# Routing of tokens in two batches instead of three, with other selection steps, and 26 extra transposes behind the attention

## The chip, the cores and the metric

The kernel runs on one core of a Trainium2 chip. TensorE (PE) multiplies and transposes and writes PSUM only; VectorE (DVE), ScalarE (ACT) and GpSimd (POOL) do the elementwise work; SyncE (SP) issues most DMAs. Every engine works through its own list in order and waits on semaphores. [...] The metric is the device time of one execution in microseconds. It was 711.97 us before, the median of 3 runs (711.90 to 711.98).

## The reference, cut to what matters

Three layers follow each other: windowed attention with sinks, a mixture of 8 experts of which each token takes two, and a gated two-layer network.

```
scores = scale * q @ k.T; keep = is_sink | in_window          # 2 x 8 heads, 768 x 64
x = softmax(where(keep, scores, -1e9)) @ v                    # becomes 1536 tokens x 512
logits = x @ w_gate
noisy = logits + log1p(exp(x @ w_noise)) * noise              # 1536 x 8
top2 = the two largest of a row, with weights softmax(top2)
for e in 8 experts: out[mask] += top2_w * (relu(x[mask] @ w1[e]) @ w2[e])
y = (h * sigmoid(h)) @ w_out, h = out @ w_in                  # 512 -> 2048 -> 512
```

## The kernel before, in words

**Attention.** The 1536 tokens are 12 blocks of 128 rows. A software pipeline goes through 48 positions (12 blocks, 4 pairs of heads each) and 12 more to drain it. At position p TensorE does the scores of p, the transposes of the exponentials of p-2 and the product with V of p-4; ScalarE does the exponentials of p-1 and the high half of the transposed part of p-3, VectorE its low half. Work that belongs to a block hangs on positions in a table, `hooks`, filled by `at(position, function, place)`. Behind the last head of a block come `fin` (the block's rows `xs`, scaled and stored to `x_d`), then `gate_block`: transposes of `xs` (`pm`), their copy `xT`, the gate product `pl`, and its copy `lg`.

**Routing.** When enough blocks have their `lg`, `route` puts a list of small VectorE steps on `drip`; one or two are taken off per position, and in the last 12 positions up to four. BATCHES makes three such lists: blocks 0 to 4, 5 to 8 and 9 to 11. A list forms the noisy logits (`noisy_top`: exponential and logarithm on ScalarE, which need two different activation tables), finds the two largest by `max` and `max_index` per block, turns them into one-hot rows `roh` and `M`, has TensorE count places (`posm`, tile `pp`), and builds two one-hot tables, `Boh` (chunk, multiplied by the token's number on GpSimd) and `Aoh` (place in the chunk). Their product `pz` (`z_part`) is the list of tokens by expert, `idx`. By `idx` GpSimd gathers the rows of the experts.

**The first 128 tokens of expert 0** can be known from the first batch alone. `f_list` finds them, a gather fetches them, `f_xt` transposes them, `f_split` makes high and low halves `fp`, and `f_l1`, `f_relu`, `f_ht`, `f_l2`, `f_out` send them through expert 0's two layers. These pieces wait in `fill` and are put by `do_fill` where TensorE would wait for the routing of the last blocks. `f_rows` then turns the other rows of expert 0, and expert 0's remaining 288 columns start (`l1` in `moe`, tile `ph`).

**Experts.** Each of the 8 experts runs 8 slices f, `l1` of one beside `l2` of the slice before (tiles `ph`, `py`). Between them stand the loads and splits of later weights (`weights_step`), the next expert's rows (`x_pair`, then a DMA transpose `x_turn` on SP's queue, tile `xT`), and the conversion of the last layer's weights (`decode_step`): an even step starts one and loads the one after next (512 KB), an odd step does two VectorE passes and stores an earlier one (256 KB, `win_d`). How many steps stand in a slice is a tuple at the end of the loop in `moe`. All these loads, stores and DMA transposes go through SP's queue in the order of the code.

Of the kernel before, what the change touches and what calls it, by code (L numbers as in the profile page):

```python
# [22 lines left out]
BATCHES = ((0, 5), (5, 9), (9, 12))  # L23
# [21 lines left out]
def setup(ctx, tc, g):  # L45
    nc = tc.nc
    g.B, g.H, g.S, g.D = g.q.shape
    g.N = g.B * g.S
    g.DM = g.H * g.D
    g.NB = g.N // 128  # L50
    g.E = g.w_gate.shape[1]
    g.F = g.w1.shape[2]
    g.F2 = g.w_out.shape[0]
    g.C = 416

    g.CT = [min(128, g.C - 128 * c) for c in range(4)]
# [12 lines left out]
    g.noise_sb = consts.tile([128, g.NB, 8], F32, name="noise_sb")  # L69
    g.ones = consts.tile([128, 128], BF16, name="ones")  # L70
    g.iota8 = consts.tile([128, 8], F32, name="iota8")
    g.M = consts.tile([128, g.NB, 8], BF16, name="M")
    g.Msum = consts.tile([128, 8], BF16, name="Msum")
    g.top8 = consts.tile([128, g.NB, 8], F32, name="top8")
    g.ix = consts.tile([128, g.NB, 8], U32, name="ix")
    g.ef = consts.tile([128, g.NB, 2], F32, name="ef")
# [12 lines left out]
    g.tops = consts.tile([128, 64], F32, name="topsl")  # L89
    g.n_sums = g.n_tops = 0  # L90
    nc.gpsimd.memset(g.sums, 0.0)


def setup_ops(tc, g):

    nc = tc.nc
    p = g.consts
    nc.gpsimd.iota(g.iota8, pattern=[[1, 8]], base=0, channel_multiplier=0,
                   allow_small_or_imprecise_dtypes=True)
    nc.gpsimd.iota(g.iotaq, pattern=[[1, 128]], base=0, channel_multiplier=0,  # L100
                   allow_small_or_imprecise_dtypes=True)
# [118 lines left out]
def noisy_top(tc, g, t, j0, j1):  # L220

    nc = tc.nc
    n = j1 - j0
    J = slice(j0, j1)
    V = nc.vector
    e, u, l, z, dd = (t("r" + c, [8]) for c in "eulzd")
    pre, nz = t("rp", [8]), t("rn", [8])
# [12 lines left out]
    add(lambda: V.tensor_scalar(z, u, 1.0, None, op0=OP.is_equal))  # L240
    add(lambda: V.scalar_tensor_tensor(dd, u, 1.0, z, op0=OP.subtract, op1=OP.add))
    add(lambda: V.tensor_mul(e, e, g.noise_sb[:, J, :]))
    add(lambda: V.reciprocal(dd, dd))
    add(lambda: V.tensor_mul(z, z, e))
    add(lambda: V.tensor_mul(dd, dd, e))
    add(lambda: V.tensor_add(pre, z, g.lg[:, J, 0:8]))
    add(lambda: V.tensor_mul(l, l, dd))
    add(lambda: V.tensor_add(nz, l, pre))
    for j in range(n):
        add(lambda j=j: V.max(g.top8[:, j0 + j, :], nz[:, j, :]))  # L250
    for j in range(n):
        add(lambda j=j: V.max_index(g.ix[:, j0 + j, :], g.top8[:, j0 + j, :], nz[:, j, :]))
    return st


def route(tc, g, wk, ps, j0, j1):
# [6 lines left out]
    def t(name, shape, dt=F32):  # L263
# [3 lines left out]
    pos = t("rpos", [2])  # L267
    sl, pm, cl = (t(c, [2], I32) for c in ("rsl", "rpm", "rcl"))
    st = noisy_top(tc, g, t, j0, j1)
    add = st.append  # L270
    add(lambda: V.tensor_tensor(oh, g.iota8[:, None, None, :].to_broadcast([128, n, 2, 8]),
                                g.ix[:, J, 0:2, None].to_broadcast([128, n, 2, 8]), op=OP.is_equal))
    add(lambda: V.tensor_add(g.M[:, J, :], oh[:, :, 0, :], oh[:, :, 1, :]))

    def posm():
        p = ps.tile([128, n, 8], F32, name="pp", tag="M")
        nc.tensor.matmul(p, g.tri, g.M[:, J, :], start=True, stop=n == 1 and j0 == 0)
        if j0:
            nc.tensor.matmul(p, g.ones, g.Msum[:, None, :].to_broadcast([128, n, 8]), start=False, stop=n == 1)
# [12 lines left out]
    add(lambda: V.tensor_reduce(pos, ps2, axis=AX.X, op=OP.add))  # L292

    add(lambda: V.scalar_tensor_tensor(sl, g.ef[:, J, :], 512.0, pos, op0=OP.mult, op1=OP.add))
# [12 lines left out]
    add(lambda: V.scalar_tensor_tensor(g.sl[:, J, :], g.ef[:, J, :], float(g.C), pos, op0=OP.mult, op1=OP.add))  # L307
    if j1 < g.NB:
        tot = wk.tile([128, 8], F32, name="rtot", bufs=1)

        def msum():
            V.tensor_reduce(tot, g.M[:, J, :].rearrange("p j e -> p e j"), axis=AX.X, op=OP.add)
            if j0:
                V.tensor_add(tot, tot, g.Msum)
            V.tensor_copy(g.Msum, tot)

        add(msum)
# [3 lines left out]
def attention(tc, g):  # L321
# [4 lines left out]
    with ExitStack() as st:  # L326
# [241 lines left out]
        keep_warm(nc, g, ps, "O", 10)  # L568
# [43 lines left out]
        for n in range(NQ):  # L612
# [39 lines left out]
        def f_split(k, scale):  # L652
# [3 lines left out]
            nc.scalar.activation(hi, p, AF.Copy, scale=scale)  # L656
# [45 lines left out]
        def f_out():  # L702
# [6 lines left out]
        work = (fl[0] + fl[1][:2] + [lambda: f_relu(0)] + fl[1][2:] + [lambda: f_ht(0), lambda: f_relu(1)] + f2[0][:2]  # L709
                + [lambda: f_ht(1)] + f2[0][2:] + f2[1] + [f_out])  # L710
# [32 lines left out]
        g.do_fill = do_fill  # L743
# [29 lines left out]
        for p in range(NP + 12):  # L773
# [196 lines left out]
def moe(tc, g, W, wk, ps):  # L970
# [98 lines left out]
    def gates():  # L1069
# [8 lines left out]
            lambda: V.tensor_sub(e2, g.top8[:, :, 1], g.top8[:, :, 0]),  # L1078
# [68 lines left out]
    for i, (e, f) in enumerate(seq):  # L1147
# [241 lines left out]
def flag_steps(tc, g, wk, ps):  # L1389
# [3 lines left out]
    t = wk.tile([128, 5], F32, name="flt", bufs=1)  # L1393
# [3 lines left out]
    def count():  # L1397
        p = ps.tile([128, 13], F32, name="pc", tag="PT")
        nc.tensor.matmul(p[:, 0:8], g.ones, g.Msum, start=True, stop=False, skip_group_check=True)
        for j in range(g.batches[-1][0], g.NB):  # L1400
            nc.tensor.matmul(p[:, 0:8], g.ones, g.M[:, j, :], start=False, stop=False, skip_group_check=True)
        nc.tensor.matmul(p[:, 8:13], g.ones, g.over, start=False, stop=True, skip_group_check=True)
        V.tensor_reduce(t[:, 0:1], p[:, 0:8], axis=AX.X, op=OP.max)
# [6 lines left out]
            lambda: V.tensor_scalar(t[:, 0:1], t[:, 0:1], float(g.C), None, op0=OP.is_gt),  # L1410
            lambda: V.tensor_scalar(t[:, 4:5], t[:, 4:5], 0.5, None, op0=OP.is_gt),
# [28 lines left out]
def general(tc, g):  # L1440
# [4 lines left out]
    with ExitStack() as ctx:  # L1445
# [72 lines left out]
        with ExitStack() as st:  # L1518
# [139 lines left out]
```

## Time and profile before

| | |
|---|---|
| median of 3 runs | 711.97 us |
| the profiled execution, whole | 713.08 us |
| its span on the core | 711.4 us |
| TensorE busy in the span | 667.1 us |
| VectorE, ScalarE, GpSimd busy | 429.3, 337.8, 214.2 us |
| mean granted clock of TensorE | 0.982 |

Rows below come from the profiled execution; its own time lies 1.11 us above the median of the runs, and 1.68 us of it lie around the span. Times in rows are microseconds from the span's start. In a row of the timeline the first two numbers are the start and the duration, `x6` says how many instructions were merged, and a bracket at the end says how long the engine was idle before and what released it.

### The profile page before, as it was taken

What the parts mean: (1) busy time and instruction counts of PE and PEld (TensorE: products, weight loads), DVE (VectorE), ACT (ScalarE), POOL (GpSimd) and SP (SyncE); (2) the same over time, 40 slices, a digit from 0 to 9 for tenths busy, and PEclk for the clock granted to TensorE, in tenths of its full rate; (3) what the DMA queues carried; (4) which work ended last, traced back from release to release, by engine and by line L of the source; (5) the groups of instructions that cost most, each with busy time, mean ns of one, the idle gap of its engine ahead of it and who ended that gap; (6) DMA issues with size and microseconds to landing.
All of it is one profiled execution on the core that took longest, in us unless ns stands there. A gap on an engine that the chain in (4) does not pass through costs nothing.

```text
span 711.4 us, 11618 instructions
## 1 busy us (share of the span) xinstructions
PE 667.1 (94%) x4292; PEld 373.1 (52%) x4292; DVE 429.3 (60%) x1091; ACT 337.8 (47%) x693; POOL 214.2 (30%) x229
## 2 busy tenths in 40 slices
PE   7999889889987999999999999899999999999993
PEld 5677667557543656565555553444444444444441
DVE  5878788737695687878797854756423344232222
ACT  4888868437663555556555441443323223222221
POOL 5868950142162162625252325222100000000000
PEclk9999999799998999999999999999999999999998
DMA  7776710539798989998894514742311011000001
GB/s 153 197 168 178 179 46 24 186 97 242 283 253 309 236 293 270 330 276 267 232 297 155 150 45 135 241 149 67 82 30 59 1 30 29 30 30 1 1 0 65
DMA packets 111682, 103.50 MB, mean 145 GB/s; under 512 B 77312, under 2 KB 77568, under 8 KB 111616
## 3 DMA queue, kind: packets, MB, share of 16 engines
q1 hardware_dynamic: 106016, 86.68, 42.4%
q0 software_dynamic: 4096, 13.11, 6.1%
q10 hardware_dynamic: 1504, 2.88, 1.1%
q8 instruction: 35, 0.57, 0.3%
q14 instruction: 31, 0.25, 0.1%
HBM read 77.29 MB, written 17.30 MB: 133 GB/s over the span
## 4 chain that ended last, share of the span: by engine, by line


## 5 line engine op out<-in xcount | busy, mean ns | idle before, releaser
L1009 PE MATMUL ph<-xT,w 128*128 128x416 f16 (+1 forms) x768 | 141.7, 335 | 8.8 <-DMA win_d<-f 6.6
L1274 PE MATMUL p<-xT,w 128*128 128x512 f16 x576 | 132.2, 379 | 2.1 <-DVE xT L1260 1.4
L1291 PE MATMUL po<-w,h 128*128 128x512 f16 x576 | 132.2, 379 | 0.0
L1025 PE MATMUL py<-h,w 128*128 128x416 f16 (+1 forms) x672 | 124.1, 331 | 3.2 <-DVE h L131 2.7
L937 POOL TENSOR_SCALAR f<-f 128x512 f32<-128x512 f32 x32 | 70.6, 2211 | 157.7 <-ACT f L936 155.6
L1009 PEld LDWEIGHTS <-w 128*128 128x128 f16 x768 | 75.4, 98 | 61.3 <-DMA win_d<-f 7.0
L1277 DVE TENSOR_TENSOR f<-p,f 128x512 f32<-128x512 f32 x48 | 33.1, 691 | 110.9 <-ACT f L1276 109.3
L1025 PEld LDWEIGHTS <-w 128*128 128x128 f16 x672 | 65.7, 98 | 52.6 <-issue 6.1
L1274 PEld LDWEIGHTS <-w 128*128 128x128 f16 x576 | 56.4, 98 | 70.1 <-issue 2.4
L1291 PEld LDWEIGHTS <-h 128*128 128x128 f16 x576 | 56.3, 98 | 67.8 <-DVE h L126 0.3
L1276 ACT ACTIVATE f<-p 128x512 f32<-128x512 f32 x48 | 28.6, 596 | 128.8 <-PE p L1274 126.5
L1012 ACT ACTIVATE h<-ph 128x416 f16<-128x416 f32 (+1 forms) x64 | 31.8, 497 | 52.0 <-PE ph L1009 51.0
L126 DVE SCALAR_TENSOR_TENSOR h<-f,h 128x512 f16<-128x512 f32 x48 | 33.2, 692 | 33.4 <-ACT h L1279 33.4
L126 DVE SCALAR_TENSOR_TENSOR w<-wst,w 128x1024 f16<-128x1024 f32 x38 | 47.2, 1245 | 8.4 <-ACT w L882 8.1
L131 DVE SCALAR_TENSOR_TENSOR h<-ph,h 128x416 f16<-128x416 f32 (+1 forms) x64 | 36.2, 566 | 24.3 <-ACT h L1012 24.3
L1279 ACT ACTIVATE h<-f 128x512 f16<-128x512 f32 x48 | 30.2, 629 | 37.8 <-DVE f L1277 37.8
L482 ACT ACTIVATE P<-pS,mx 128x260 f32<-128x260 f32 (+1 forms) x96 | 43.0, 458 | 1.9 <-DVE mx L473 1.6
L882 ACT ACTIVATE w<-wst 128x1024 f16<-128x1024 f32 x38 | 39.6, 1047 | 0.0
L126 DVE SCALAR_TENSOR_TENSOR rows<-xg,rows 128x512 f16<-128x512 f32 (+1 forms) x36 | 24.8, 688 | 24.2 <-ACT rows L988 24.1
L980 POOL DMA_INDIRECT xg<-x_d,idx x28 | 32.6, 1166 | 20.5 <-DVE topsl L121 13.5
L1064 ACT ACTIVATE yo<-tpy 128x512 f32<-128x512 f32 (+1 forms) x27 | 16.1, 595 | 45.4 <-PE tpy L1054 29.6
L126 DVE SCALAR_TENSOR_TENSOR w<-rows,w 128x1024 f16<-128x1024 f32 x26 | 31.9, 1231 | 4.4 <-ACT w L882 4.1
(254 smaller groups left out, 956.1 us busy)
## 6 DMA issues: line engine op xcount, KB each, us to landing
wst<-in_moe_w_dram SPq DMA_DIRECT2D x42, 512.0 KB
rows<-in_moe_w_dram SPq DMA_DIRECT2D x22, 512.0 KB
f<-in_moe_w_in_dram SPq DMA_DIRECT2D x16, 512.0 KB
f<-in_moe_w_out_dram SPq DMA_DIRECT2D x16, 512.0 KB
y_d<-yo SPq DMA_DIRECT2D x23, 256.0 KB
rawv<-in_v_dram SPq DMA_DIRECT2D x12, 256.0 KB
x_d<-xs SPq DMA_DIRECT2D x12, 256.0 KB
rows<-in_k_dram SPq DMA_DIRECT2D x11, 256.0 KB
```

Of the source, the lines that this page charges most:

```text
L126: nc.vector.scalar_tensor_tensor(o, x, scale, hi, op0=OP.mult, op1=OP.subtract, accum_out=sum_at(g)[:o.shape[0]] if check else None)
L131: nc.vector.scalar_tensor_tensor(o, x, 0.0, hi, op0=OP.max, op1=OP.subtract, accum_out=sum_at(g))
L482: nc.scalar.activation(Pt[n][:, h, :wd], psS[pr][:, a, :wd], AF.Exp, bias=nmx[pr][:, a:a + 1], accum_out=sm[n][:, h:h + 1])
L882: nc.scalar.activation(self.u[u][k][0][:, 2 * h:2 * h + 2, :], st["t"], AF.Copy, scale=scale)
L937: nc.gpsimd.tensor_scalar(a, a, 2.0 ** -15, 2.0 ** -80, op0=OP.max, op1=OP.mult)
L980: nc.gpsimd.indirect_dma_start(out=t[:CT[c]], out_offset=None, in_=g.x_d[:, :], in_offset=bass.IndirectOffsetOnAxis(ap=g.idx[:CT[c], 4 * e ...
L1009: nc.tensor.matmul(p[:, v], w[x][:, d, c], xT[e][y][:, d, v], start=d == 0 and k == 0, stop=d == 3 and k == 2)
L1012: nc.scalar.activation(hi[:, v], p[:, v], AF.Relu)
L1025: nc.tensor.matmul(ys[e][d][:, v], w[x][:, f % 4, d * 128:(d + 1) * 128], h[y][:, v], start=f == 0 and k == 0, stop=f == 7 and k == 2)
L1274: nc.tensor.matmul(p, w[x][:, d, c], xT[q][y][:, d, :], start=z == 0, stop=z == 11)
L1277: V.tensor_mul(s, p, s)
L1291: nc.tensor.matmul(po[q][t], h[x][:, 128 * t:128 * t + 128], w[y][:, f % 4, :], start=f == 0 and k == 0, stop=f == 15 and k == 2)
```

## The change

It has four parts.

1. BATCHES becomes two batches of six blocks. The second starts one position earlier than the last one did.
2. The steps of a list change. The logarithm's division by (u - 1) is made safe by adding a tiny number, without the mask `z`. The two largest are found for all blocks at once by a reduction and a comparison, twice. The expert's offset (512 per expert) sits in the start value of the running count `Msum`, so that the position product gives the slot itself.
3. Behind the attention, TensorE gets four sets of 128x128 transposes of the identity (`warm`: 8, 6, 2, 10). `f_xt` and the pieces of `fill` move to fixed places; the high half of `fp` for the first tokens goes from ScalarE to VectorE; the second layer of the first 128 tokens stands ahead of `f_rows` now, and `f_out` comes last.
4. The tuple of `decode_step`: expert 1 has 7 steps instead of 10, every later expert 10 (before: 9 for even, 10 for odd ones). The number is 67 in all, as before.

The check of the token counts (`flag_steps`) takes off the new start value and has two steps more.

```diff
-BATCHES = ((0, 5), (5, 9), (9, 12))
+BATCHES = ((0, 6), (6, 12))
...
-    add(lambda: V.tensor_scalar(z, u, 1.0, None, op0=OP.is_equal))
-    add(lambda: V.scalar_tensor_tensor(dd, u, 1.0, z, op0=OP.subtract, op1=OP.add))
+    add(lambda: V.tensor_scalar(dd, u, -1.0, TINY, op0=OP.add, op1=OP.add))
     add(lambda: V.tensor_mul(e, e, g.noise_sb[:, J, :]))
     add(lambda: V.reciprocal(dd, dd))
-    add(lambda: V.tensor_mul(z, z, e))
-    add(lambda: V.tensor_mul(dd, dd, e))
-    add(lambda: V.tensor_add(pre, z, g.lg[:, J, 0:8]))
-    add(lambda: V.tensor_mul(l, l, dd))
-    add(lambda: V.tensor_add(nz, l, pre))
-    for j in range(n):
-        add(lambda j=j: V.max(g.top8[:, j0 + j, :], nz[:, j, :]))
-    for j in range(n):
-        add(lambda j=j: V.max_index(g.ix[:, j0 + j, :], g.top8[:, j0 + j, :], nz[:, j, :]))
+    add(lambda: V.scalar_tensor_tensor(l, l, TINY, dd, op0=OP.add, op1=OP.mult))
+    add(lambda: V.tensor_mul(l, l, e))
+    add(lambda: V.tensor_add(nz, l, g.lg[:, J, 0:8]))
...
+    def pick(k):
+        m = g.top2[:, J, k]
+        add(lambda: V.tensor_reduce(m, nz, axis=AX.X, op=OP.max))
+        add(lambda: V.tensor_tensor(oh[:, :, k, :], nz, m[:, :, None].to_broadcast([128, n, 8]), op=OP.is_equal))
+    pick(0)
+    add(lambda: V.scalar_tensor_tensor(nz, oh[:, :, 0, :], -3e38, nz, op0=OP.mult, op1=OP.add))
+    pick(1)
...
             if n == NQ - 1:
-                at(e + 5, lambda: do_fill(2))
+                at(e + 3, lambda: warm(8))
+                at(e + 4, lambda: warm(6))
+                at(e + 5, lambda: warm(2))
+                at(e + 7, lambda: (f_xt(), warm(10)))
+                at(e + 8, lambda: do_fill(5))
+                at(e + 10, lambda: do_fill(5))
...
-            nc.scalar.activation(hi, p, AF.Copy, scale=scale)
+            if k:
+                nc.scalar.activation(hi, p, AF.Copy, scale=scale)
+            else:
+                nc.vector.tensor_scalar(hi, p, scale, None, op0=OP.mult)
...
+        def warm(n):
+            for x in range(n):
+                nc.tensor.transpose(zt[1][:, x % 4, :], g.idf, g.idf)
...
+        do_fill(len(fill))
+        f_ht(0)
         z_part(g.batches[-1][0], NB)
         z = zt[0]
         nc.vector.tensor_scalar(g.idx, z, float(g.N - 1), None, op0=OP.min)
         f_gather()
-        do_fill(len(fill) - 5)
+        for f in f2[0][:2] + [lambda: f_ht(1)] + f2[0][2:] + f2[1]:
+            f()
+        for f in g.after:
+            f()
         f_rows(1)
         f_rows(2)
-        do_fill(1)
         f_rows(3)
-        do_fill(len(fill))
+        f_out()
...
-        for _ in range((0, 1, 1, 1, 1, 1, 2, 2)[f] + (f == 4 and e % 2) if e else 0):
+        for _ in range(((0, 1, 1, 1, 1, 1, 1, 1), (0, 1, 1, 1, 1, 2, 2, 2))[e > 1][f] if e else 0):
             decode_step(dstep[0])
```

TensorE before, from the last block's attention (`pO` with the sinks `skT`) into the first layer of the first 128 tokens (`pf` with the weights `w`); `pm` and `pl` are the last block's gate, `pp` the count of the second batch:

```order
L556 MATMUL pO<-Vs_126,skT 128x512
L675 MATMUL pf_2584<-idf,rows_101 128x128 x4
L203 MATMUL pm<-idf,xs 128x128 x4
...
L277 MATMUL pp<-M,tri 128x32
...
L212 MATMUL pl<-wgn,xT 128x16 x4
...
L682 MATMUL pf_2614<-w_375,fp_203 128x512
```

The same place in the change; `pz` from `idf` are the new transposes:

```order
L558 MATMUL pO<-Vs_124,skT 128x512
L780 MATMUL pz<-idf 128x128 x8
L206 MATMUL pm<-idf,xs 128x128 x4
L780 MATMUL pz<-idf 128x128 x6
L215 MATMUL pl<-wgn,xT 128x16 x4
L780 MATMUL pz<-idf 128x128 x2
L686 MATMUL pf_2599<-idf,rows_99 128x128 x4
L780 MATMUL pz<-idf 128x128 x10
...
L693 MATMUL pf_2621<-w_374,fp_201 128x512
```

The count `pp` of the middle batch no longer stands between `pm` and `pl`, and the transposes fill the places in front of `pm`, `pl` and the first layer.

VectorE in the change, from the last block's `lg` to the reduction that picks the largest:

```order
L218 COPY lg<-pl 128x16
L239 TENSOR_SCALAR ru<-re 128x48
L242 TENSOR_SCALAR rd<-ru 128x48
L243 TENSOR_TENSOR re<-re,noise_sb 128x48
L667 TENSOR_SCALAR fp_201<-pf_2599 128x4x128
L129 SCALAR_TENSOR_TENSOR fp_202,sumsl<-pf_2599,fp_201 128x4x128
L244 RECIPROCAL rd<-rd 128x48
L245 SCALAR_TENSOR_TENSOR rl<-rl,rd 128x48
L246 TENSOR_TENSOR rl<-rl,re 128x48
L247 TENSOR_TENSOR rn<-rl,lg 128x48
L269 TENSOR_REDUCE top_77<-rn 128x6
```

Both halves of `fp` stand inside the last batch's list now; before, the low half alone stood there, inside the middle batch's `max_index` steps.

SP's queue in expert 1 before, from the third DMA transpose for expert 2 on (`xT`; the piece of 32 rows is the last of four):

```order
L1369 DMA_TRANSPOSE xT<-rows_101 128x8x128
L877 DMA wst<-in_moe_w_dram 128x2x512
L962 DMA win_d<-f_3339 128x512
L1067 DMA y_d<-yo 32x512
L1369 DMA_TRANSPOSE xT<-rows_101 128x8x32
L877 DMA wst<-in_moe_w_dram 128x2x512
L931 DMA f_3519<-in_moe_w_out_dram 128x1024
L962 DMA win_d<-f_3400 128x512
```

The same place in the change:

```order
L1385 DMA_TRANSPOSE xT<-rows_99 128x8x128
L893 DMA wst<-in_moe_w_dram 128x2x512
L947 DMA f_3407<-in_moe_w_out_dram 128x1024
L1083 DMA y_d<-yo 32x512
L1385 DMA_TRANSPOSE xT<-rows_99 128x8x32
L893 DMA wst<-in_moe_w_dram 128x2x512
L978 DMA win_d<-f_3295 128x512
L893 DMA rows_100<-in_moe_w_dram 128x2x512
```

The store `win_d` of 256 KB that stood ahead of the last transpose comes behind it, and the load `f` of 512 KB shown there stood ahead of the third transpose before.

## Rows read from the trace of the kernel before

**Rows 1.** The page, part 1: TensorE's busy time, share of the span, instructions.
```profile
PE 667.1 (94%) x4292; PEld 373.1 (52%) x4292; DVE 429.3 (60%) x1091; ACT 337.8 (47%) x693; POOL 214.2 (30%) x229
```

**Rows 2.** Waits of TensorE: who waited for whom, us in total, times, longest.
```profile
PE ph L1009 <- DMA win_d<-f: 6.6, 1, 6.6
```

**Rows 3.** Stretches: length, busy of each engine (x), granted clock, DMA share, GB/s.
```profile
96.00:98.00 2.00, 2.00 (x13) 1.12 (x11) 1.77 (x5) 1.66 (x6) 1.94 (x3) 0.50 0.47 108
...
128.00:130.00 2.00, 1.60 (x14) 1.22 (x11) 1.80 (x15) 0.42 (x1) 0.00 (x0) 0.87 0.15 55
130.00:139.00 9.00, 7.51 (x44) 4.05 (x44) 6.85 (x38) 4.00 (x7) 0.98 (x1) 0.50 0.95 321
...
212.00:218.50 6.50, 0.00 (x0) 0.02 (x1) 4.86 (x14) 0.59 (x1) 0.00 (x0) 0.72 1.02 275
```

**Rows 4.** Timeline of TensorE behind the attention.
```profile
119.31 1.04 PE L212 MATMUL pl<-wgn,xT 128*128 128x16 f32 x8
...
129.38 1.04 PE L203 MATMUL pm<-idf,xs 128*128 128x128 f32 x4
...
132.21 1.89 PE L212 MATMUL pl<-wgn,xT 128*128 128x16 f32 x8 [0.31 <-DVE rps L288]
133.94 2.72 PE L682 MATMUL pf<-w,fp 128*128 128x512 f16 x6
...
146.09 0.60 PE L692 MATMUL pf<-idf,rows 128*128 128x128 f32 x4
146.52 1.46 PE L699 MATMUL pf<-w,fp 128*128 128x512 f16 x6
147.82 0.60 PE L727 MATMUL pf<-idf,rawv 128*128 128x128 f32 x4
...
154.34 3.10 PE L1009 MATMUL ph<-xT,w 128*128 128x288 f16 x24 [1.89 <-ACT Aoh L704]
```

**Rows 5.** Timeline of TensorE: starts of the scores at five positions of the attention.
```profile
80.79 0.39 PE L463 MATMUL pS<-MA,idb 128*128 128x260 bf16 x2
84.74 0.38 PE L463 MATMUL pS<-MA,idb 128*128 128x260 bf16 x2 [0.84 <-ACT P L482]
...
91.61 0.39 PE L463 MATMUL pS<-MA,idb 128*128 128x260 bf16 x2
95.83 0.64 PE L463 MATMUL pS<-MA,idb 128*128 128x260 bf16 x2
99.32 0.39 PE L463 MATMUL pS<-MA,idb 128*128 128x260 bf16 x2
```

**Rows 6.** Timeline of ScalarE: loads of an activation table.
```profile
82.37 1.28 ACT L482 ACT_TABLE_LOAD   x1
...
124.20 1.28 ACT L238 ACT_TABLE_LOAD   x1
```

**Rows 7.** Timeline of VectorE: steps of the routing.
```profile
86.42 0.95 DVE L242 TENSOR_TENSOR re<-re,noise_sb 128x40 f32<-128x40 f32 x1
...
128.64 0.67 DVE L563 TENSOR_TENSOR xs<-pO,rs 128x512 f32<-128x512 f32 x1
...
134.13 0.17 DVE L215 COPY lg<-pl 128x16 f32<-128x16 f32 x1 [1.25 <-PE pl L212]
...
137.29 0.18 DVE L242 TENSOR_TENSOR re<-re,noise_sb 128x24 f32<-128x24 f32 x1
...
141.70 1.33 DVE L303 TENSOR_TENSOR Aoh<-iotaq,rpm 128x512 f16<-128x512 f32 x2
...
143.34 0.19 DVE L813 TENSOR_SCALAR idx<-pz 128x32 int32<-128x32 f32 x1 [0.23 <-PE pz L763]
```

**Rows 8.** Timeline of GpSimd: the first gather by `idx`.
```profile
143.80 0.98 POOL L717 DMA_INDIRECT rawv<-x_d,idx  x1 [1.05 <-PE pf L692]
```

**Rows 9.** Timeline of SP's queue: the last DMA transpose for expert 2.
```profile
207.79 1.18 SPq L1369 DMA_TRANSPOSE xT<-rows  x1
```

**Rows 10.** Timeline of TensorE at the start of expert 2.
```profile
218.51 3.80 PE L1009 MATMUL ph<-xT,w 128*128 128x416 f16 x12 [6.64 <-DMA win_d<-f]
```

More of the change, by code (lines that the diff above doesn't have):

```diff
@@ L22 @@
 PSC = 4096.0
-BATCHES = ((0, 5), (5, 9), (9, 12))
+TINY = 1e-30
+BATCHES = ((0, 6), (6, 12))
 SX, SW1, SW2 = 2.0 ** 8, 2.0 ** 9, 2.0 ** 9
@@ L70, in setup @@
     g.ones = consts.tile([128, 128], BF16, name="ones")
-    g.iota8 = consts.tile([128, 8], F32, name="iota8")
     g.M = consts.tile([128, g.NB, 8], BF16, name="M")
     g.Msum = consts.tile([128, 8], BF16, name="Msum")
-    g.top8 = consts.tile([128, g.NB, 8], F32, name="top8")
-    g.ix = consts.tile([128, g.NB, 8], U32, name="ix")
-    g.ef = consts.tile([128, g.NB, 2], F32, name="ef")
+    g.start = consts.tile([128, 8], F32, name="startl")
+    g.top2 = consts.tile([128, g.NB, 2], F32, name="top2")
     g.sl = consts.tile([128, g.NB, 2], F32, name="sl")
@@ L97, in setup_ops @@
     p = g.consts
-    nc.gpsimd.iota(g.iota8, pattern=[[1, 8]], base=0, channel_multiplier=0,
+    nc.gpsimd.iota(g.start, pattern=[[512, 8]], base=0, channel_multiplier=0,
                    allow_small_or_imprecise_dtypes=True)
+    nc.gpsimd.tensor_scalar(g.Msum, g.start, 1.0 / 128, 1.0, op0=OP.mult, op1=OP.mult)
     nc.gpsimd.iota(g.iotaq, pattern=[[1, 128]], base=0, channel_multiplier=0,
@@ L217, in gate_block, with noisy @@
     return a, b, c, d
-def noisy_top(tc, g, t, j0, j1):
+def noisy(tc, g, t, j0, j1):
     nc = tc.nc
-    n = j1 - j0
     J = slice(j0, j1)
     V = nc.vector
-    e, u, l, z, dd = (t("r" + c, [8]) for c in "eulzd")
-    pre, nz = t("rp", [8]), t("rn", [8])
+    e, u, l, dd, nz = (t("r" + c, [8]) for c in "euldn")
     st = []
@@ L276, in posm @@
         p = ps.tile([128, n, 8], F32, name="pp", tag="M")
-        nc.tensor.matmul(p, g.tri, g.M[:, J, :], start=True, stop=n == 1 and j0 == 0)
-        if j0:
-            nc.tensor.matmul(p, g.ones, g.Msum[:, None, :].to_broadcast([128, n, 8]), start=False, stop=n == 1)
+        nc.tensor.matmul(p, g.tri, g.M[:, J, :], start=True, stop=False)
+        nc.tensor.matmul(p, g.ones, g.Msum[:, None, :].to_broadcast([128, n, 8]), start=False, stop=n == 1)
         for k in range(n - 1):
@@ L291, in route, with slots @@
     add(posm)
-    add(lambda: V.tensor_reduce(pos, ps2, axis=AX.X, op=OP.add))
-    add(lambda: V.scalar_tensor_tensor(sl, g.ef[:, J, :], 512.0, pos, op0=OP.mult, op1=OP.add))
+    def slots():
+        with nc.allow_low_precision(reason="whole numbers below 8192"):
+            V.tensor_reduce(sl, ps2, axis=AX.X, op=OP.add)
+    add(slots)
     add(lambda: V.tensor_scalar(cl, sl, 7, None, op0=OP.logical_shift_right))
@@ L306, in route @@
                                              op=OP.is_equal))
-    add(lambda: V.scalar_tensor_tensor(g.sl[:, J, :], g.ef[:, J, :], float(g.C), pos, op0=OP.mult, op1=OP.add))
+    add2 = add if j1 < g.NB else g.after.append
+    add2(lambda: V.tensor_scalar(cl, sl, 9, None, op0=OP.logical_shift_right))
+    add2(lambda: V.scalar_tensor_tensor(g.sl[:, J, :], cl, float(g.C - 512), sl, op0=OP.mult, op1=OP.add))
     if j1 < g.NB:
@@ L565, in fin @@
             xsd[n] = xs
-        keep_warm(nc, g, ps, "O", 10)
+        keep_warm(nc, g, ps, "S", 10)
         numbers_load(tc, g, one)
@@ L708, in attention @@
         f2 = [[lambda u=u, d=d: f_l2(u, d) for d in range(4)] for u in range(2)]
-        work = (fl[0] + fl[1][:2] + [lambda: f_relu(0)] + fl[1][2:] + [lambda: f_ht(0), lambda: f_relu(1)] + f2[0][:2]
-                + [lambda: f_ht(1)] + f2[0][2:] + f2[1] + [f_out])
+        work = fl[0] + [lambda: f_relu(0)] + fl[1] + [lambda: f_relu(1)]
         def f_gather():
@@ L1187, in moe @@
         if i == 7:
-            dec[0][0]()
-            dec[1][0]()
-        for _ in range((0, 1, 1, 1, 1, 1, 2, 2)[f] + (f == 4 and e % 2) if e else 0):
+            for n in range(2):
+                dec[n][0]()
+        for _ in range(((0, 1, 1, 1, 1, 1, 1, 1), (0, 1, 1, 1, 1, 2, 2, 2))[e > 1][f] if e else 0):
             decode_step(dstep[0])
@@ L1392, in flag_steps @@
     V = nc.vector
-    t = wk.tile([128, 5], F32, name="flt", bufs=1)
+    t = wk.tile([128, 6], F32, name="flt", bufs=1)
+    cn = wk.tile([128, 8], F32, name="flc", bufs=1)
     g.flag = g.consts.tile([128, 1], I32, name="flag")
@@ L1402, in count @@
         nc.tensor.matmul(p[:, 8:13], g.ones, g.over, start=False, stop=True, skip_group_check=True)
-        V.tensor_reduce(t[:, 0:1], p[:, 0:8], axis=AX.X, op=OP.max)
+        V.tensor_sub(cn, p[:, 0:8], g.start)
+        V.tensor_reduce(t[:, 0:1], cn, axis=AX.X, op=OP.max)
+        V.tensor_reduce(t[:, 5:6], cn, axis=AX.X, op=OP.add)
         V.tensor_reduce(t[:, 4:5], p[:, 8:13], axis=AX.X, op=OP.max)
@@ L1532, in t @@
                 return wk.tile([128, NB] + shape, F32, name="g" + name)
-            for f in noisy_top(tc, g, t, 0, NB):
-                f()
+            nz, st_ = noisy(tc, g, t, 0, NB)
+            for f in st_:
+                f()
+            top8, ix = t("top8", [8]), wk.tile([128, NB, 8], U32, name="gix")
+            for j in range(NB):
+                V.max(top8[:, j, :], nz[:, j, :])
+                V.max_index(ix[:, j, :], top8[:, j, :], nz[:, j, :])
+            iota8 = wk.tile([128, 8], F32, name="giota8")
+            nc.gpsimd.iota(iota8, pattern=[[1, 8]], base=0, channel_multiplier=0,
+                           allow_small_or_imprecise_dtypes=True)
             gt = wk.tile([128, 2, NB], F32, name="ggt")
-            V.tensor_sub(gt[:, 1], g.top8[:, :, 1], g.top8[:, :, 0])
+            V.tensor_sub(gt[:, 1], top8[:, :, 1], top8[:, :, 0])
             nc.scalar.activation(gt[:, 1], gt[:, 1], AF.Exp)
```

36 lines of the change are left out of this document (13 added, 23 removed).

## The prediction

> **What bounds the kernel now.** I read the page first: TensorE is busy for 94% of the span [rows 1], so only places where it waits or runs at its low clock are worth anything. Its list of waits gives one long wait, 6.6 us at the start of expert 2 [rows 2]. [...]
>
> *Behind the attention.* From the scaled rows of the last block (`xs`, 128.64) to its logits (`lg`, 134.13) pass 5.49 us, from there to the list `idx` (143.34) 9.21, and from there to expert 0's first matmul (154.34) 11.0 [rows 4, 7]. The clock falls between 128 and 130, where TensorE is busy for 1.60 of 2 us, and stays low for 9 us of 84% busy time [rows 3]. Six matmuls of the first layer take 2.72 us there and 1.46 at the high level [rows 4].
>
> *In the attention.* A position takes 2.29 us (three of them from 84.74 to 91.61). Two take 3.95 and 4.22, from 80.79 and from 91.61, and the one behind the second 3.49, at the low clock [rows 3, 5]. The first of them holds a pair of table loads of 1.28 us each, of which the second is shown [rows 6]; they belong to the first batch's logarithm. The second holds VectorE's routing steps, which are slow while GpSimd works: a product of 40 words takes 0.95 us at 86.42, one of 24 words 0.18 at 137.29 [rows 7].
>
> *At expert 2.* Its last DMA transpose is issued at 207.79, TensorE starts at 218.51, and the DMA engines are fully busy in between [rows 3, 9, 10]. This is a queue that is full, not an engine that is late.
>
> **The change part by part.** The sum is made against the profiled execution of 713.08 us.
>
> *Start of the tail: -0.6.* The middle batch's logarithm loaded its table at 124.20, ahead of the last two copies of the attention on ScalarE [rows 6]. That load of 1.28 us is gone from there. What is put in its way is the token product of the first six blocks, 12 small matmuls ahead of the last product with V; I charge half of the load for these and for waits on other engines. Bounds: 0 and -1.3.
>
> *`xs` to `lg`: -2.2.* The parts are `xs` 0.67, four transposes 0.60, the copy of 512 columns (taken at the length of `xs`, 0.67), the gate product 1.04 at the high clock, and handovers of 0.3 in all: 3.3 us against 5.49 [rows 4, 7]. Before, the same transposes took 1.04 and the product 1.89, and the count of the middle batch stood between them. The new transposes cost nothing here if the clock is high: four take 0.43 from start to start (146.09 to 146.52, rows 4), so 8 take 0.9, beside the 0.7 of `xs`, and 6 take 0.65, beside the copy.
>
> *`lg` to `idx`: +1.0.* This gets longer, because six blocks instead of three are routed behind the last logits. Exponential, table load, a dummy and the logarithm: 2.05 us [rows 6]. VectorE meanwhile does the four new steps of `fp` and the list, and with both halves of `fp` (0.7 each, by `xs`) and the reciprocal is ready at 2.65. Nine dependent steps up to the one-hot `M` follow; such a step takes 0.18 or 0.19 [rows 7], with the handover 0.24: 4.8. By the same step length I put the count on TensorE at 0.55 and the five steps to `Boh` at 1.35; then six blocks of `Aoh` at 0.44 each (1.33 for three, rows 7), 2.65: 9.35. The low half of the first hidden part stands ahead of `idx` and waits for ScalarE's high half: 0.75. That is 10.2 against 9.21. The ten transposes (1.1 us) lie beside the two halves of `fp`, the 24 first-layer matmuls (0.24 each, rows 4) beside the rest.
>
> *`idx` to expert 0: -2.2.* Of the 24 matmuls of the second layer 22 remain at `idx`: 5.3 us. Transposes of the second hidden part take 0.45, then come those of the gathered rows. The gather is in time: before it was asked for at 143.80 and taken 4.0 us later without a wait [rows 4, 8]; the work ahead of it is now 5.8 us. From the first gathered transposes (0.6) a copy on ScalarE (0.7) and three low halves on VectorE (0.7, 0.7 and 0.2 for a quarter of the columns) lead to the first matmul: 8.75 us against 11.0. Before, nine matmuls and `f_out` stood behind the rows, and TensorE waited 1.89 us for that copy [rows 4]; now it lies beside the low halves.
>
> *In the attention: -2.0.* The first batch starts four positions later. The position from 80.79 loses its two table loads and falls from 3.95 to about 2.4. The one from 91.61 gets them, but it was already 4.22 long, and keeps that. Later steps meet less of GpSimd's work and are fewer (21 small ones instead of 31 or so); 0.5 for that. Whether the 1.2 us behind (3.49 against 2.29, rows 5) come back with the clock I leave out. Bounds: 0, if the pair costs at its new place what it saves, and -4.
>
> *At expert 2: -0.9.* One store of 256 KB leaves the queue ahead of the last transpose; at 275 GB/s [rows 3] that is 0.95 us of a wait of 6.6. The load of 512 KB shown beside it stays ahead of that transpose. If transfers of the same queue share the engines instead of following each other, the load that no longer stands behind it counts too: -3. If the earlier loads fill the gap: +0.5. I take the order of the queue.
>
> *The rest: 0.* The ten added steps of the check and the larger count lie on VectorE beside the matmuls of the slices; where VectorE is full they move a weight split by as long as they take, ten times 0.18 at most. The new tuple gives experts 2, 4 and 6 one decode step more ahead of their last transpose, see below.
>
> Sum: -0.6 - 2.2 + 1.0 - 2.2 - 2.0 - 0.9 = -6.9, so 706.2 for a profiled execution. The median of the runs lies 1.11 us below the profiled one: **705.1 us**.
>
> [...] The clock fell between 128 and 130 while TensorE did eight 128x128 transposes back to back [rows 3, 4]; no row shows transposes alone holding the high level. [...]
>
> **The rivals.**
>
> *The clock falls all the same.* For it: the row just named. Against it: from 84.74 to 91.61 every position holds four transposes, waits included, and the scores keep their 0.38 of the high level [rows 5]. Price, from rows 4: the gate's transposes +0.45 and product +0.85, `f_xt` +0.45, the ten transposes +1.1, 12 first-layer matmuls +2.6 (0.45 instead of 0.24 each), ahead of which the count cannot run. This is 5.5: 710.6 us.
>
> *The attention gives nothing back.* The table loads stall the position from 91.61 as they did the one from 80.79, on top of the slow steps. For it: GpSimd is as busy there (1.94 of 2 us, rows 3). Against it: ScalarE's loads and VectorE's slow steps can run beside each other, so the longer of them counts, not their sum. 2.0 less: 707.1.
>
> *A new wait between experts, slower.* Experts 2, 4 and 6 put 512 KB or a store more ahead of the next expert's last transpose, and two steps stand in slice 5. If one boundary fills up as expert 2's did, it costs that wait of 6.6 and the half-speed matmuls behind it (3.80 against 2.4 us, by the 1.46 of rows 4 and the width of 416): 8.0, so 713.1. It decides from a wait of 6.9 us on. Against it: expert 3 had as many steps, and the list of waits has no second long one [rows 2].
>
> **How the numbers follow.** Forecast 0.60, clock falls 0.20, attention gives nothing 0.10, new wait 0.10. What this measurement can tell from no change is 0.2%, 1.4 us. The forecast and the third case lie below 710.5; the clock case straddles it, with 0.16 faster, 0.02 same, 0.02 slower; the new wait is slower at 0.09. That gives faster 0.84, same 0.05, slower 0.11. The forecast's own range is 702 to 708, from the bounds of the attention and of expert 2. Widened to the clock case it is 702 to 711; above it lie the new wait and some of the clock case, below it the outermost bounds.
>
> **What would show it.** Granted clock 1.00 from 128 us to expert 0; `xs` to `lg` in 3.3 us, `lg` to `idx` in 10, expert 0 about 4 us nearer to the last scores; the position with the table loads near 4.2 us, the one four before it near 2.4; expert 2's wait at 5.5 to 6. Wrong would be: 0.50 behind the attention, a position near 6 us, or a second long wait on a DMA in the experts.

## The result and the profile after

The changed kernel took **705.58 us** (median of 4 runs, 705.41 to 705.92), against 711.98 us before (4 runs, 711.90 to 712.12): a ratio of 0.9911, 95% interval 0.9893 to 0.9928, 6.4 us faster. The profiled execution took 705.41 us, its span is 703.7 us. The forecast was 705.1. The number came out and most of the signs did; the experiments show that the reason was another one.

First the signs, in the order of the groups of before. The page's first part:

```profile
PE 664.9 (94%) x4323; PEld 373.4 (53%) x4323; DVE 424.8 (60%) x1035; ACT 335.2 (48%) x688; POOL 213.4 (30%) x229
```

TensorE has 2.2 us less to do than before [rows 1], so some 5.5 of the 7.7 us of span that went were waiting. The stretches after [as rows 3; the last is TensorE's wait at expert 2]:

```profile
96.00:98.00 2.00, 1.47 (x15) 1.01 (x16) 2.00 (x5) 1.51 (x5) 2.00 (x3) 1.00 0.00 0
128.00:130.00 2.00, 1.97 (x18) 1.73 (x17) 0.26 (x2) 0.62 (x3) 0.00 (x0) 1.00 0.89 252
130.00:139.00 9.00, 8.13 (x60) 4.40 (x58) 8.07 (x25) 3.32 (x6) 1.20 (x1) 1.00 0.71 256
204.90:210.70 5.80, 0.04 (x1) 0.03 (x1) 2.77 (x10) 0.00 (x0) 4.24 (x4) 0.82 1.05 278
```

The granted clock, which the profile gives as a share, stays at 1.00 from 128 to 139 us, where it was 0.50 from 130 on. TensorE's timeline there and at expert 2 [as rows 4 and 10], `pz<-idf` being the new transposes:

```profile
125.73 0.48 PE L558 MATMUL pO<-Vs,skT 128*128 128x512 f32 x1
126.04 1.03 PE L780 MATMUL pz<-idf 128*128 128x128 f32 x8
...
128.33 1.06 PE L215 MATMUL pl<-wgn,xT 128*128 128x16 f32 x8
...
131.10 3.07 PE L693 MATMUL pf<-w,fp 128*128 128x512 f16 x12
...
145.77 0.99 PE L737 MATMUL pf<-idf,rawv 128*128 128x128 f32 x8 [0.71 <-DMA rawv<-x_d,idx]
148.10 3.10 PE L1025 MATMUL ph<-xT,w 128*128 128x288 f16 x24 [1.34 <-DVE xT L129]
...
210.70 4.32 PE L1025 MATMUL ph<-xT,w 128*128 128x416 f16 x12 [5.75 <-issue]
```

The product `pl` takes 1.06 instead of 1.89, twelve first-layer matmuls 3.07 (six took 2.72), and expert 0 starts 6.24 us earlier. Expert 2 still waits 5.75 us, and its first twelve matmuls take 4.32 instead of 3.80. VectorE [as rows 7]:

```profile
126.24 0.69 DVE L565 TENSOR_TENSOR xs<-pO,rs 128x512 f32<-128x512 f32 x1 [0.80 <-PE pO L558]
129.44 0.17 DVE L218 COPY lg<-pl 128x16 f32<-128x16 f32 x1 [2.50 <-PE pl L215]
...
131.69 0.45 DVE L244 RECIPROCAL rd<-rd 128x48 f32<-128x48 f32 x1
...
134.17 0.21 DVE L275 TENSOR_TENSOR M<-roh 128x48 bf16<-128x48 f32 x1
...
136.05 2.52 DVE L304 TENSOR_TENSOR Aoh<-iotaq,rpm 128x512 f16<-128x512 f32 x3
...
139.13 0.18 DVE L827 TENSOR_SCALAR idx<-pz 128x32 int32<-128x32 f32 x1
```

`xs` to `lg` takes 3.20 us, `lg` to `idx` 9.69, `idx` to expert 0 8.97. Last, the scores in the attention [as rows 5], and ScalarE's table loads [as rows 6]:

```profile
81.09 0.39 PE L465 MATMUL pS<-MA,idb 128*128 128x260 bf16 x2
83.27 0.39 PE L465 MATMUL pS<-MA,idb 128*128 128x260 bf16 x2
...
89.90 0.39 PE L465 MATMUL pS<-MA,idb 128*128 128x260 bf16 x2
93.51 0.38 PE L465 MATMUL pS<-MA,idb 128*128 128x260 bf16 x2 [0.83 <-ACT P L484]
...
118.46 0.38 PE L465 MATMUL pS<-MA,idb 128*128 128x260 bf16 x2
```

```profile
88.61 1.28 ACT L240 ACT_TABLE_LOAD   x1
91.14 1.28 ACT L484 ACT_TABLE_LOAD   x1
129.90 1.28 ACT L236 ACT_TABLE_LOAD   x1
```

The position from 81 takes 2.18 us, the one with the table loads 3.61, and no load stands ahead of the attention's last copies.

### The profile page after: what moved, and what is told of

Its sections match the earlier page's. It is cut to its first block, busy times and chain, and to the rows that moved or that the text cites. A ratio compares the mean times of both kernels' runs of the same rounds, so it can differ in the third digit from the quotient of the medians.

```text
span 703.7 us, 11622 instructions
## 1 busy us (share of the span) xinstructions
PE 664.9 (94%) x4323; PEld 373.4 (53%) x4323; DVE 424.8 (60%) x1035; ACT 335.2 (48%) x688; POOL 213.4 (30%) x229
## 4 chain that ended last, share of the span: by engine, by line
## 5 line engine op out<-in xcount | busy, mean ns | idle before, releaser
L996 POOL DMA_INDIRECT xg<-x_d,idx x28 | 30.8, 1100 | 18.5 <-DVE topsl L124 11.5
```

The source lines that it names most:

```text
L996: nc.gpsimd.indirect_dma_start(out=t[:CT[c]], out_offset=None, in_=g.x_d[:, :], in_offset=bass.IndirectOffsetOnAxis(ap=g.idx[:CT[c], 4 * e ...
```

## The experiments

Three groups of four kernels ran, each group on one chip beside the kernel before. On these chips the executions of one kernel lie some 2 to 9 us apart, two lone outliers left aside, so kernels are compared by their ratio to the kernel before of the same group; "us" is the median.

| run | ratio to before (95%) | us (before) |
|---|---|---|
| e1_no_transposes | 0.9911 (0.9879 to 0.9942) | 706.50 (712.94) |
| e2_three_batches | 0.9965 (0.9939 to 0.9991) | 709.90 |
| e3_old_tuple | 0.9993 (0.9975 to 1.0011) | 712.63 |
| e4_late_catchup | 0.9900 (0.9866 to 0.9934) | 706.09 |
| e5_changed_again | 0.9923 (0.9902 to 0.9944) | 706.33 (710.95) |
| e6_before_new_tuple | 0.9906 (0.9888 to 0.9924) | 704.17 |
| e7_catchup_spread | 0.9846 (0.9822 to 0.9869) | 699.66 |
| e8_spread_no_transposes | 0.9861 (0.9841 to 0.9882) | 701.27 |
| e9_before_spread | 0.9891 (0.9866 to 0.9915) | 705.17 (713.62) |
| e10_spread_again | 0.9860 (0.9826 to 0.9893) | 702.18 |
| e11_spread_hold | 0.9872 (0.9847 to 0.9896) | 703.69 |
| e12_before_spread_two | 0.9930 (0.9906 to 0.9955) | 708.17 |

**The tuple, put back and put in alone.**

```diff
# e3, in the changed kernel (e6: the reverse, in the kernel before)
-        for _ in range(((0, 1, 1, 1, 1, 1, 1, 1), (0, 1, 1, 1, 1, 2, 2, 2))[e > 1][f] if e else 0):
+        for _ in range((0, 1, 1, 1, 1, 1, 2, 2)[f] + (f == 4 and e % 2) if e else 0):
```

> The changed kernel with the decode steps spread as before (expert 1 ten, later experts nine and ten). Theory A (the queue's order ahead of the last DMA transpose of expert 2 sets the wait): one store of 256 KB is back ahead of it, the wait at expert 2 goes from 5.75 to 6.7 us, 706.5 us (706.2 to 706.9). Rival B (the wait follows from all bytes asked for in expert 1): three more steps put 1 MB more on the engines, 2.5 us or more longer, 708 us. Rival C (the gap is set elsewhere): no change, 705.6 us.

> The kernel before with the new tuple of decode steps alone. Theory A (expert 2's start is held by a DMA queue that runs on its own clock, so TensorE's gains ahead of it and the bytes ahead of it are not two terms of a sum): expert 0 starts near 154 us as before, its wait at expert 2 falls from 6.6 to between 1 and 2.5 us, 707 us (706 to 709). Theory B (the forecast's term, one store of 256 KB): the wait falls by 0.9 us, 711.1 us. Rival C (the tuple brings nothing without the faster tail): 712 us.

> The changed kernel itself, as the measure for the kernels beside it on the same chip. Theory A: its time is set by the DMA queue ahead of expert 2, so its wait there lies between 5 and 8 us and the time follows the wait: 705.6 us with 5.8 us, more with more. Theory B (the terms of the forecast add up): 0.990 of the kernel before, whatever the wait.

These make a square: neither part 1.0000, the rest of the change without the tuple 0.9993, the tuple without the rest 0.9906, both 0.9923 (0.9911 in the first result). **The tuple alone gives the whole gain; the new tail, the batches and the transposes give none at the end**, though expert 0 starts at 148.19 us in e3 as in e5, 6 us ahead of before. The price of 0.9 us for the tuple is refuted, and so is the sum. TensorE at expert 2 in e3, then in e6:

```profile
217.94 3.99 PE L1025 MATMUL ph<-xT,w 128*128 128x416 f16 x12 [10.30 <-DMA win_d<-f]
```

```profile
211.01 2.27 PE L1009 MATMUL ph<-xT,w 128*128 128x416 f16 x12 [1.43 <-DMA y_d<-yo]
```

With the old tuple expert 2 starts at 218 whether expert 0 starts at 148 (e3) or 154 (before); the six microseconds are waited away. e3's size met none of its theories (706.5, 708 and 705.6 against 712.6). In e6 theory A had the wait right and the time too high (704.17, below its 706 to 709). The table puts the executions with such a wait side by side (us; the timelines of TensorE and SP's queue; the last column is the share of GpSimd's queue in the DMA view, times the stretch from the last DMA transpose to expert 2's start):

| | expert 0 | last transpose issued | expert 2 | its wait | first gather issued | gathers on the DMA engines |
|---|---|---|---|---|---|---|
| before (old tuple) | 154.34 | 207.79 | 218.51 | 6.64 | 204.53 | 4.3 |
| e3 (old tuple) | 148.19 | 205.35 | 217.94 | 10.30 | 200.23 | 5.0 |
| after | 148.10 | 201.14 | 210.70 | 5.75 | 202.63 | 1.5 |
| e5 (after again) | 148.19 | 202.37 | 213.00 | 6.28 | 204.34 | 2.7 |
| e2 | 153.05 | 205.87 | 213.70 | 3.88 | 207.49 | 1.1 |
| e1 | 152.30 | 207.21 | 213.79 | 2.66 | 208.66 | 0.0 |
| e6 | 151.55 | 205.20 | 211.01 | 1.43 | 207.20 | 0 |

With the new tuple expert 2 starts at 211 to 214 whatever expert 0 does. The last two columns show a part that I had not looked at: GpSimd's gathers of expert 3's rows. The queues in the stretch from the last DMA transpose to expert 2's start (packets, MB, share of the 16 engines; q1 holds the transfers issued by SP, q0 GpSimd's gathers), before, then after, then e6:

```profile
q1 hardware_dynamic: 2187, 2.01, 67.5%
q0 software_dynamic: 272, 0.85, 39.7%
```

```profile
q1 hardware_dynamic: 2098, 1.98, 94.2%
q0 software_dynamic: 113, 0.40, 15.4%
```

```profile
q1 hardware_dynamic: 2170, 2.12, 109.2%
```

And GpSimd before, then after:

```profile
201.63 2.74 POOL L937 TENSOR_SCALAR f<-f 128x512 f32<-128x512 f32 x1 [2.05 <-ACT f L936]
204.53 1.24 POOL L980 DMA_INDIRECT xg<-x_d,idx  x1 [0.16 <-issue]
```

```profile
199.84 2.63 POOL L953 TENSOR_SCALAR f<-f 128x512 f32<-128x512 f32 x1 [6.49 <-ACT f L952]
202.63 1.03 POOL L996 DMA_INDIRECT xg<-x_d,idx  x1 [0.16 <-issue]
```

The gathers stand in GpSimd's list behind the third piece of the decode. The new tuple starts that piece a slice later, so the gathers come 1.5 us behind the last transpose instead of 3.3 us ahead of it, and hold the engines for 1.5 us of that stretch instead of 4.3. That fits the two rows with the old tuple against the five with the new one, but it is a comparison of traces and not shown: a kernel that moves the gathers alone was not run. Two things speak against giving the gathers too much. In all five rows with the new tuple the first gather is issued 1.45 to 2.0 us behind the last transpose, and the longer the stretch is, the more of the gathers falls into it; there the last column can be a consequence of the wait as well as its cause. And in e9 below (old tuple, no wait at expert 2) the gathers are issued 1.5 us ahead of the last transpose too (203.03 and 204.50). A rival stands untested: the new tuple also moves a load of 512 KB from ahead of the third transpose to behind it. Nor are the gathers the whole: in the changed kernel q1's transfers hold the engines for 9.0 us (94.2% of 9.56) where before they held them for 7.2.

**The bytes ahead of the transposes.** Weight pieces (512 KB each, loaded and split) are taken on one per slice; from slice 2 of expert 1 on the loop takes three more. e4 takes these in expert 2, e7 one each in experts 3, 4 and 5.

```diff
-            if done[0] < (i if i < 10 else i + 3):
+            if done[0] < (i if i < 18 else i + 3):                        # e4
+            if done[0] < i + (i >= 24) + (i >= 32) + (i >= 40):           # e7, e8, e9, e10, e11, e12
```

> The changed kernel; the three additional pieces of expert weights (512 KB each, loads with their splits) which the loop takes on in slices 2 to 5 of expert 1 are taken on eight slices later, in expert 2. Theory A (expert 2's wait is a full queue ahead of its last DMA transpose, and these loads fill it): 1.5 MB at 275 to 395 GB/s is 4 to 5.7 us off a wait of 5.75 us, and the first 12 matmuls behind it run at the high clock (2.3 instead of 4.3 us); nothing new at expert 3, since later experts had no such wait with as many decode steps; 699 us (698 to 701.5). Rival B (the same bytes meet the transposes of expert 3): a wait of 5 us there, 705.6 us. Rival C (the splits of these pieces on VectorE, not the bytes, fill expert 1): the wait shrinks by under 1.5 us, 704.5 us.

> The changed kernel; the three additional pieces of expert weights of 512 KB each, which the loop takes on in slices 2 to 5 of expert 1, are taken on one by one in the first slice of experts 3, 4 and 5. Theory A (bytes ahead of the transposes): no wait over 1 us at expert 2 and none at expert 3, since no expert has more than one piece added and it comes before its transposes; the 12 matmuls behind both run at the high clock; 5.75 us of waiting and 2.0 us of half speed are gone: 698 us (697 to 700). Rival B (the decode's bytes meet the same pieces later): a wait of 3 us or more at expert 3, 4 or 5, 702 us or more.

> The changed kernel with spread pieces, again, as the measure for the kernels beside it on the same chip: 0.985 of the kernel before, 699.7 us. Its profile before this one had the clock at 0.50 for about 2 us at expert 0's start and again at the end; where neither falls, 698 us or less.

In e4 the wait at expert 2 is gone and one of 4.17 us comes at expert 3, rival B's place; the median (706.09, executions from 700.37 to 708.94) shows little gain. In e7 there is no wait at either, at expert 2:

```profile
205.29 2.27 PE L1041 MATMUL py<-h,w 128*128 128x416 f16 x12
207.40 2.27 PE L1025 MATMUL ph<-xT,w 128*128 128x416 f16 x12
```

Theory A is borne out: with these pieces out of the way of expert 2's transposes its wait is gone. The edit moves the splits on VectorE together with the loads; during the wait in the changed kernel the DMA engines are full (share 1.05) while VectorE is busy for 2.77 of 5.80 us, which speaks for the bytes, but the two were not moved apart. e7 is the fastest kernel here, 6.7 us under the changed kernel of its group (699.66 against 706.33); e10 repeats it at 0.9860, its fastest execution 699.30, its median (702.18) above the 699.7 expected.

**The rest of the change with the queue relieved.**

> The kernel before (old tuple, old tail, three batches) with the three additional weight pieces spread over experts 3, 4 and 5. Theory A (bytes ahead of expert 2's transposes made its wait, and the tail's gain shows once the wait is gone): no wait over 1 us at expert 2, the 12 matmuls behind it at the high clock; 711 - 6.6 - 1.5 = 703 us (702 to 704.5), 3 to 6 us above the changed kernel with spread pieces. Rival B (new tail, batches and transposes are worth nothing even so): the same time as the changed kernel with spread pieces, within 1 us. Rival C (the old tuple alone fills the queue): a wait of 4 us or more at expert 2, 708 us or more.

e9 has no wait at expert 2 either, and stands at 705.17, a little above theory A's range; e10 in the same group is 3.0 us faster. So the rest is worth some 3 us (the intervals overlap, and e10 has the new tuple too) once nothing behind it waits for the queue, against the 6.0 that the forecast gave it.

**The transposes.** e1 and e8 leave them out, without and with the spread.

```diff
-            for x in range(n):
+            for x in range(0):
                 nc.tensor.transpose(zt[1][:, x % 4, :], g.idf, g.idf)
```

> The changed kernel (705.6 us) without its 26 identity transposes; all else stays where it is. Theory A (they hold TensorE's clock): the granted clock falls to 0.50 behind the attention as it did before the change, from xs to lg pass about 4.4 us instead of 3.2, twelve or more first-layer matmuls take 0.45 us each instead of 0.24; expert 0 starts about 4 us later; 709.5 us (708 to 711). Rival B (the order of the tail alone made the gain and the transposes are lost time): clock 1.00 or low without harm, 705.6 us or up to 0.5 less. Rival C (the clock falls for xs to lg only, and the first-layer matmuls bring it back): 706.8 us.

> The kernel with the spread pieces without the 26 identity transposes. Without the spread the transposes made expert 0 start 3.7 us earlier, but the wait at expert 2 was 3.1 us shorter without them. Theory A (the wait at expert 2 had hidden their gain): with no wait there the whole of it shows, 701.7 us (701 to 702.5), 3.7 us above the kernel with transposes and pieces spread. Rival B (the first layer's half-speed start is made up elsewhere): 698.5 us.

The stretches behind the attention and at expert 0's start, columns as in rows 3, of e1, e8, e5 and e10:

```profile
126.00:146.00 20.00, 17.31 (x99) 9.24 (x96) 10.36 (x33) 4.86 (x9) 3.58 (x4) 0.74 0.46 159
```

```profile
126.00:146.00 20.00, 17.27 (x97) 9.29 (x94) 10.31 (x33) 4.85 (x9) 4.70 (x5) 0.83 0.53 172
```

```profile
126.00:146.00 20.00, 18.43 (x126) 11.24 (x124) 10.37 (x34) 5.45 (x10) 5.91 (x6) 1.00 0.55 183
146.00:152.00 6.00, 4.72 (x27) 3.08 (x28) 2.14 (x9) 1.67 (x4) 1.81 (x2) 0.73 0.51 157
```

```profile
126.00:146.00 20.00, 18.63 (x135) 11.43 (x132) 10.30 (x33) 5.28 (x10) 5.91 (x6) 1.00 0.55 179
146.00:152.00 6.00, 4.71 (x39) 3.71 (x40) 2.33 (x10) 2.42 (x7) 1.82 (x3) 1.00 0.55 175
```

They do hold the clock: it is 1.00 from 126 to 146 us in all 8 profiles with the transposes and falls to 0.50 there in all 6 without (0.66 to 0.91 in the mean of these 20 us), of which e1 and e8 lack nothing but the transposes. What that is worth varies. From `xs` to expert 0 pass 25.5 us in e1 and 22.8 in e8, against 21.3 to 21.9 in six profiles with the transposes (without e2 and e11). At the end little is left: e1 equals the changed kernel, because its wait at expert 2 is 3.1 us shorter; e8 comes near theory A's figure (701.27), but it lies 1.6 us above e7, the same kernel with the transposes in its group, where 3.7 were expected, the intervals overlap, and its ratio equals that of e10; so a gain at the end isn't shown.

**More transposes.** In two of the 8 profiles (e5, e7) the clock falls at expert 0 instead (0.73 and 0.72 from 146 to 152 us), behind TensorE's wait of 1.3 us; in five others it holds at 1.00 behind a wait of 1.3 to 1.5 us at the same place. e11 fills that place:

```diff
+        warm(6)
         f_rows(1)
         f_rows(2)
         f_rows(3)
         f_out()
+        warm(10)
```

> The changed kernel with spread pieces and 16 identity transposes more: 6 ahead of the gathered rows, where TensorE waits 0.7 us for the gather, and 10 ahead of expert 0, where it waits 1.3 us for VectorE. Theory A (the wait ahead of expert 0 is what lets the clock fall in some executions, 4.7 instead of 3.1 us for the first 24 matmuls): clock 1.00 from 128 to 160 us, 0.5 to 1.5 us less in the median than without them, 698.5 us. Rival B (the clock falls there for another reason): no change, 699.7 us. Rival C (they delay the matmuls behind them): up to 0.5 us more.

```profile
146.77 1.31 PE L780 MATMUL pz<-idf 128*128 128x128 f32 x10
150.27 2.00 PE L1027 MATMUL ph<-xT,w 128*128 128x288 f16 x15 [2.20 <-ACT Aoh L715]
```

Rival C: the clock holds (1.00 from 126 to 152 us, which, by those five, says little of the added transposes), but expert 0 starts 11.3 us behind `idx` instead of 8.7 in e10, because ScalarE's three copies of the gathered rows start 1.6 to 3 us later after `idx`; what holds them behind transposes that they don't need was not followed. The median is 1.5 us above e10's, where rival C had up to 0.5 (the intervals overlap).

**The batches.** e2 puts three batches into the changed kernel, e12 two into the kernel before (the line BATCHES, and the tile `pz` claimed when the scores have left its place).

> The changed kernel with the three batches of before (blocks 0 to 4, 5 to 8, 9 to 11); the new steps, the transposes and the tail's order stay. Theory A (two batches gave the attention's gain): the position near 81 us is long again (3.9 instead of 2.2), a logarithm's table load stands again ahead of the last copies of the attention, last scores about 2 us later (120.4 instead of 118.5); in the tail three blocks instead of six save about 1.3 us of one-hot rows between lg and idx (8.4 instead of 9.7); 706.9 us (705.8 to 708.5). Rival B (the shorter steps gave the attention's gain, the number of batches nothing): last scores near 118.6, tail shorter, 704.3 us. Rival C (the middle batch comes into the tail again and holds up the gate product): xs to lg above 4 us, 709 us.

> The kernel before with spread pieces and two batches of six blocks, with its old steps and its old tail. Theory A (the batches, not the shorter steps, shorten the attention): last scores 1.5 to 3 us earlier than with three batches, no table load ahead of the last copies; in the tail six blocks cost about 2.3 us more between lg and idx (six more searches of 0.17 us, three one-hot blocks of 0.44 us): 702 us (700.5 to 703.5) where three batches give 703. Rival B (the steps shorten it): last scores as with three batches, 705 us.

Scores in e2, then in e12:

```profile
81.55 0.39 PE L465 MATMUL pS<-MA,idb 128*128 128x260 bf16 x2
85.49 0.38 PE L465 MATMUL pS<-MA,idb 128*128 128x260 bf16 x2 [0.83 <-ACT P L484]
...
118.77 0.39 PE L465 MATMUL pS<-MA,idb 128*128 128x260 bf16 x2
122.88 0.38 PE L465 MATMUL pS<-MA,idb 128*128 128x260 bf16 x2 [1.27 <-ACT P L484]
```

```profile
81.94 0.38 PE L463 MATMUL pS<-MA,idb 128*128 128x260 bf16 x2
84.12 0.39 PE L463 MATMUL pS<-MA,idb 128*128 128x260 bf16 x2
...
118.76 0.38 PE L463 MATMUL pS<-MA,idb 128*128 128x260 bf16 x2
```

From the position near 81 to the last scores: 41.3 us in e2, 36.8 in e12, 37.2 to 37.4 in the changed kernel (after, e5, e10), 38.3 to 39.4 in before, e6 and e9. The batches shorten the attention, not the steps, as theory A has it. e2 is some 3 to 4 us slower than the changed kernel (0.9965 against 0.9911 and 0.9923; its interval just touches the second one's), more than the 1.3 expected: its tail saves little (`lg` to `idx` 9.19 instead of 9.69 us; 8.4 was expected). And e12 as a whole is 3.0 us slower than e9: with the old tail the first tokens' rows come late (TensorE waits 2.7 us for their gather) and the clock is at 0.50 from 128 to 140 us. My 702 missed this by 6 us.

## Why the prediction was right and wrong

- *The number* (705.1 against 705.58) and the signs asked for came out, save the position with the table loads (3.61 us, not 4.2). The time was right by a wrong reason, which is luck.
- *Start of the tail and attention* (-0.6, -2.0). In the two profiles the last scores come 1.75 us earlier although the attention began 0.3 us later, and 0.65 goes behind them. The mechanism is shown by e2 and e12. The size was partly that one execution's: the low clock from 96 to 98 us [rows 3] is 1.00 in e6 and e9, which run the same instructions there; against these the attention gains 1.1 us. The slow steps beside GpSimd are seen after too: a product of 48 words takes 0.65 us at 92.77, where GpSimd works, and 0.20 at 130.24, where it is idle; the reciprocal takes 0.45 at both places (95.19 and 131.69).
- *The tail*. `xs` to `lg` 3.20 (3.3 forecast) and `idx` to expert 0 8.97 (8.75) hold. `lg` to `idx` was set half a microsecond too high (9.69, not 10.2). The gather was not quite in time: TensorE waited 0.71 us for it. Here too one execution stood for all: `xs` to expert 0 takes 25.7 us before, 23.2 in e6 and 24.4 in e9.
- *Expert 2* (-0.9): **this is the step that failed.** The wait fell by 0.89 us, as priced, but only because two larger effects met: the tuple alone takes 5.2 us off it (6.64 to 1.43 in e6), and earlier arrival alone adds 3.7 (10.30 in e3). I took the wait as a term beside the tail's, while expert 2's start follows the queues and not TensorE; and I priced the tuple by one store of 256 KB on SP's queue. I did not follow it through GpSimd's list, where it moved the gathers past the last transpose; how much of the 5.2 us is theirs, and how much that of the store and the load on SP's queue, stays open.
- *The sum* therefore came out of terms that don't add: -6.0 for the rest and -0.9 for the tuple, where the runs give -0.5 us (e3, 0.07% of 712.94) and -6.7 us (e6, 0.94% of 710.95) for each alone.
- *The rivals.* "The clock falls all the same" is refuted by 8 profiles: after, 18 transposes in a row (8 and 6 of the identity, 4 of `xs`) ran from 126.04 to 128.33 us and the clock stayed at 1.00 behind them, where e1 and e8, without the 26, fell to 0.50. "The attention gives nothing back" is refuted by the position with the table loads, which takes 3.61 us and so less than the 4.22 before, while the one that lost them takes 2.18. "A new wait, slower" did not come: the old one stayed.
- *Slips*: the prediction speaks of ten added steps of the check, the section on the change of two; the diff adds three on VectorE, and the term was zero either way. The parts of `lg` to `idx` add up to 10.1, not 10.2, those of `idx` to expert 0 to 8.7, not 8.75, the twelve matmuls of the first rival cost 2.5, not 2.6, and the chances for faster add up to 0.86, not 0.84. TensorE's 7.51 of 9 us is 83%. None of this changes the forecast by more than 0.2 us.

## What to carry to other kernels

Where a wait on a full queue stands downstream, a gain upstream of it isn't a term of a sum (here expert 2 started at 218 us whether expert 0 started at 148 or 154): price the queue first, and run each half of such a change alone, since the two traces of before and after can look as if everything had added up. A step that is moved must be followed through every engine's list, also into what merely stands behind it there (here four gathers behind one GpSimd step). A duration that hangs on the clock is read from several executions, not from one (here `xs` to expert 0 took 25.7, 23.2 and 24.4 us with the same instructions).

## What the runs showed of the hardware

The clock falls behind the attention at different times in executions of the same instructions (in e6 and e9 the first lower stretch of 2 us is that from 132, with 0.72 and 0.80, before it is the one from 128, with 0.87) and stays low for different lengths, some 3.5 us in e6 and 10 before. The DMA engines were once fully busy and moved little: in e3, from 204 to 210 us, DMA transposes, gathers and the other transfers together show a share of 1.18 at 150 GB/s, where in e6 the same stretch has 1.07 at 369 GB/s.
